# Batch 0's scores and the head of its softmax in two halves of the tokens

## Chip, core and metric

One core of a Trainium2 chip runs the kernel alone. The metric is the device time of one execution in microseconds (us). In the profile of the kernel before, TensorE carries the matrix multiplications and transposes (4265 records), VectorE and ScalarE the work on elements (744 and 415), and SyncE issues the transfers (116). The mean clock that TensorE was granted is its share of full speed, 1.00 being full. Each experiment was timed in rounds beside the kernel before; there were three sets of rounds, on three different chips.

## The reference, cut to what matters

```python
# x: (8, 8, 512, 64), state: (8, 8, 32, 64)
scores = scale * x @ state.T          # softmax over the 32 states
xread  = softmax(scores) @ state
scores2 = scale * state @ x.T         # softmax over the 512 tokens
sread  = softmax(scores2) @ x
# both, concatenated along the tokens -> (4352, 512)
h = y @ w_in                          # 512 -> 2048
out = (h * sigmoid(1.702 * h)) @ w_out
```

## The kernel before

The weights arrive as 8-byte words and are rounded on the chip to fp32 in "pieces". `w_in` has four column blocks of four pieces each. A piece takes a load, a "power" (`L182` on VectorE, then `L187` and `L188` on ScalarE) and four VectorE instructions (`L197` to `L200`). The product of batch 0's state with the first column block, called M, needs pieces 0 to 3. The first useful large matmuls, h, need M and batch 0's softmax.

```python
def att_xT_arriving(b, warm):                # transposes of x, chunk by chunk as it lands
    for c in range(SCH):                     # 4 chunks of 128 tokens
        keep_warm(warm)                      # fillers: matmuls on zeros, results unused
        ps = att_ps([P, NPR, P], ...)
        for j in range(NPR):
            nc.tensor.transpose(ps[:, j], x_heads(b, c, j), ident)
        (nc.scalar.copy if c % 2 else nc.vector.tensor_copy)(A[b]["xT"][...], ps)
...
att_xT_arriving(0, 2)
att_scores(0)
powers_to(2)          # power of piece 1
att_blocks(0)         # L285: 32x32 transposes of the scores
att_x_exp(0)          # L321 maximum, L322 subtraction, L323 exponential
round_to(2, 1)        # power of piece 2, rounding of piece 1
att_x_norm(0)         # L330 sum ... L335
keep_warm(24)
att_state(1)
... transposes of batch 1's x ...
att_scores(1)
keep_warm(24)
powers_to(4)
round_to(NPR, 2)      # pieces 2 and 3
att_M(0, 0)           # M
```

Of the kernel before, what the change touches and what calls it, by code (L numbers as in the profile page):

```python
# [10 lines left out]
FP32 = mybir.dt.float32  # L11
I32 = mybir.dt.int32
U32 = mybir.dt.uint32
AF = mybir.ActivationFunctionType
ALU = mybir.AluOpType
AX = mybir.AxisListType
# [4 lines left out]
def kernel(  # L21
# [30 lines left out]
    nc = tc.nc  # L52

    B, H, S, D = x.shape
    Ns = state.shape[2]
    DM = H * D
    DF = moe_w_in.shape[1]
    P = 128
    NPR = P // Ns
    NG = H // NPR  # L60
# [5 lines left out]
    NB = S // Ns  # L66
    HF, HN = NF // 2, DM // 2
    scale = float(1.0 / np.sqrt(D))
# [10 lines left out]
    apool = ctx.enter_context(tc.tile_pool(name="apool", bufs=1))  # L79
# [4 lines left out]
    psH = ctx.enter_context(tc.tile_pool(name="psH", bufs=2, space=bass.MemoryType.PSUM))  # L84
    psO = ctx.enter_context(tc.tile_pool(name="psO", bufs=4, space=bass.MemoryType.PSUM))
# [3 lines left out]
    def att_ps(shape, name):  # L89
        return psA.tile(shape, FP32, tag="att", name=name)  # L90
# [21 lines left out]
    def keep_warm(n):  # L112
        ps = psH.tile([P, FC], FP32, tag="h", name="warm")
        for _ in range(n):
            nc.tensor.matmul(ps, zeros[:, :P], zeros, start=True, stop=True)
# [17 lines left out]
    def x_heads(b, c, j):  # L133
        return xn[b][:, c, NG * j : NG * (j + 1)].rearrange("q g d -> q (g d)")
# [33 lines left out]
    for i, v in enumerate((8.0 * most, 8.0 * (most - least))):  # L168
        t = konst.tile([P, 1], FP32, name=f"edge_{i}")
# [45 lines left out]
    def powers_to(n):  # L215
        while done["a"] < min(n, len(PIECES)):
            load_weights(done["a"] + 1)
            round_a(done["a"])
            done["a"] += 1

    def round_to(n, ahead=AHEAD):

        while done["b"] < min(n, len(PIECES)):
            powers_to(min(done["b"] + 1 + ahead, max(NFC * NPR, done["b"] + 1)))
            round_b(done["b"])
            done["b"] += 1
            while done["b"] > NPR and done["load"] < len(PIECES) and before(done["load"]) < done["b"]:
                load_weights(done["load"] + 1)
# [12 lines left out]
    A = {b: {} for b in range(B)}  # L241

    def att_state(b):
        ps = att_ps([P, P], f"stT_{b}")
        nc.tensor.transpose(ps, stn[b].rearrange("p g d -> p (g d)"), ident)
        A[b]["stT"] = apool.tile([P, P], FP32, tag="stT", name=f"stT_{b}", bufs=2)
        nc.scalar.copy(A[b]["stT"], ps)
# [9 lines left out]
    def att_xT_arriving(b, warm):  # L257

        A[b]["xT"] = apool.tile([P, NPR, S], FP32, tag="xT", name=f"xT_{b}")
        for c in range(SCH):  # L260
            keep_warm(warm)
            ps = att_ps([P, NPR, P], f"xT_{b}_{c}")
            for j in range(NPR):
                nc.tensor.transpose(ps[:, j], x_heads(b, c, j), ident)
            (nc.scalar.copy if c % 2 else nc.vector.tensor_copy)(A[b]["xT"][:, :, P * c : P * (c + 1)], ps)

    def by_state(b, ps, rhs):

        for j in range(NPR):
            for g in range(NG):  # L270
                rows, st = slice(D * g, D * (g + 1)), slice(Ns * j, Ns * (j + 1))
                nc.tensor.matmul(ps[g][st], A[b]["stT"][rows, st], rhs(rows, j), start=True, stop=True)  # L272

    def att_scores(b):
        a = A[b]
        a["s"] = [psO.tile([P, S], FP32, tag="o", name=f"s_{b}_{g}") for g in range(NG)]
        by_state(b, a["s"], lambda rows, j: a["xT"][rows, j])

    def att_blocks(b):

        a = A[b]
        t = apool.tile([P, NG, NB, Ns], FP32, tag="e1", name=f"e1_{b}")
        a["e1"] = t
        for g in range(NG):
            nc.vector.transpose(t[:, g].rearrange("p i n -> p (i n)"), a["s"][g])  # L285
# [30 lines left out]
    def att_x_exp(b):  # L316

        a = A[b]
        t = a["e1"].rearrange("p g i n -> p (g i) n")
        mx = apool.tile([P, NS1], FP32, tag="mx", name=f"mx_{b}")  # L320
        nc.vector.reduce_max(out=mx, in_=t, axis=AX.X)  # L321
        nc.vector.tensor_tensor(out=t, in0=t, in1=mx.to_broadcast((P, NS1, Ns)), op=ALU.subtract)  # L322
        nc.scalar.activation(out=t, in_=t, func=AF.Exp, scale=scale)  # L323
# [15 lines left out]
    def att_M(b, c, spare=False):  # L339

        m = mpool.tile([P, NG, FC], FP32, tag="M", name=f"M_{b}_{c}")
        A[b]["M", c] = m
        name = f"M_{b}_{c}_"
        ps = [psH.tile([P, FC], FP32, tag="h", name=name + str(g)) if spare else att_ps([P, FC], name + str(g)) for g in range(NG)]
        by_state(b, ps, lambda rows, j: w_in[c][rows, j])
        for g in range(NG):
            nc.scalar.copy(m[:, g], ps[g])  # L347
# [337 lines left out]
    round_to(1, 0)  # L685
    att_state(0)
    att_xT_arriving(0, 2)
    att_scores(0)
    powers_to(2)
    att_blocks(0)  # L690
    att_x_exp(0)
    round_to(2, 1)
    att_x_norm(0)
    keep_warm(24)
# [2 lines left out]
        keep_warm(2)  # L697
        att_xT(1, j)
    att_scores(1)
    keep_warm(24)  # L700
    powers_to(4)
    round_to(NPR, 2)
    att_M(0, 0)
# [130 lines left out]
```

## Time and profile before

| | before |
|---|---|
| time, median of the first 3 runs | 754.42 us (754.26 to 754.55) |
| TensorE, VectorE, ScalarE busy | 738.5, 432.5, 233.1 us of 752.6 |
| mean granted clock, profiled run | 0.999 |
| M starts; h starts | 29.31; 31.15 us |

TensorE is busy 98% of the time, so the end should move with the moment at which its useful work begins. The relevant stretch is the first 43 us; in the timelines, columns are start, duration, engine, line, operation, and in brackets how long the engine was idle before it and what ended that. PE stands for TensorE, DVE for VectorE, ACT for ScalarE. The prediction shows the lines.

### The profile page before, as it was taken

What the parts mean: (1) busy time and instruction counts of PE and PEld (TensorE: products, weight loads), DVE (VectorE), ACT (ScalarE), POOL (GpSimd) and SP (SyncE); (2) the same over time, 40 slices, a digit from 0 to 9 for tenths busy, and PEclk for the clock granted to TensorE, in tenths of its full rate; (3) what the DMA queues carried; (4) which work ended last, traced back from release to release, by engine and by line L of the source; (5) the groups of instructions that cost most, each with busy time, mean ns of one, the idle gap of its engine ahead of it and who ended that gap; (6) DMA issues with size and microseconds to landing.
All of it is one profiled execution on the core that took longest, in us unless ns stands there. A gap on an engine that the chain in (4) does not pass through costs nothing.

```text
span 752.6 us, 10076 instructions
## 1 busy us (share of the span) xinstructions
PE 738.5 (98%) x4265; PEld 564.6 (75%) x4267; DVE 432.5 (57%) x744; ACT 233.1 (31%) x415; POOL 0.8 (0%) x8
## 2 busy tenths in 40 slices
PE   8989999999999999999999999999999999999997
PEld 3433444467888878887788788887888778888996
DVE  5999799642646383645637264638355563762341
ACT  4676511022324241433134232424143313300210
POOL 0000000000000000000000000000000000000000
PEclk9999999999999999999999999999999999999999
DMA  9811245010030000300030003000030000000000
GB/s 234 332 57 56 93 160 144 0 57 1 28 86 4 1 15 31 72 1 15 29 74 0 1 29 84 6 1 15 29 74 1 15 29 15 0 15 29 15 1 28
DMA packets 48764, 35.24 MB, mean 47 GB/s; under 512 B 36432, under 2 KB 44112, under 8 KB 48720
## 3 DMA queue, kind: packets, MB, share of 16 engines
q1 hardware_dynamic: 48720, 34.61, 16.0%
q8 instruction: 33, 0.54, 0.3%
q14 instruction: 11, 0.09, 0.0%
HBM read 25.69 MB, written 8.91 MB: 46 GB/s over the span
## 4 chain that ended last, share of the span: by engine, by line
PE 96%; SPq 2%; ACT 1%; DMA 1%; issue 0%; DVE 0%; ACTq 0%
PE y L483 19%; PE z L483 13%; PE x L483 13%; PE upy L614 8%; PE h L418 8%; PE o L436 7%; PE upz L614 6%; PE upx L614 6%; PE M L272 4%; PE xT L254 2%; PE upy_sr L614 1%; PE y_sr L483 1%; SPq L131 1%; PE sr L367 1%; PE s L272 1%; PE upz_sr L614 1%
## 5 line engine op out<-in xcount | busy, mean ns | idle before, releaser
L483 PE MATMUL x<-w_out,g 128*128 128x256 f32 x448 | 100.2, 379 | 0.0
L483 PEld LDWEIGHTS x<-w_out,g 128*128 128x128 f32 x448 | 84.3, 190 | 11.2 <-ACT osb L443 0.2
L624 DVE TENSOR_TENSOR g<-upy,g 128x512 f32<-128x512 f32 x72 | 48.1, 689 | 68.4 <-PE upy L614 68.4
L621 ACT ACTIVATE g<-g 128x512 f32<-128x512 f32 (+1 forms) x84 | 49.8, 600 | 100.5 <-DVE g L624 100.5
L347 ACT COPY M<-M 128x512 f32<-128x512 f32 x64 | 33.2, 596 | 95.1 <-PE M L272 95.1
L418 PE MATMUL h<-aT,M 128*128 128x512 f32 x128 | 58.2, 600 | 4.4 <-ACT M L347 4.4
L418 PEld LDWEIGHTS h<-aT,M 128*128 128x128 f32 x128 | 23.6, 190 | 36.7 <-issue 24.4
L483 PE MATMUL z<-sums,later 128*128 128x256 f32 x224 | 51.1, 382 | 0.0
L483 PE MATMUL z<-w_out,g 128*128 128x256 f32 x224 | 50.8, 382 | 0.0
L483 PE MATMUL y<-sums,later 128*128 128x256 f32 x224 | 50.5, 379 | 0.0
L483 PE MATMUL y<-sums,g 128*128 128x256 f32 x224 | 50.5, 379 | 0.0
L483 PE MATMUL y<-w_out,g 128*128 128x256 f32 x224 | 50.1, 382 | 0.0
L483 PEld LDWEIGHTS z<-sums,later 128*128 128x128 f32 x224 | 42.1, 190 | 10.4 <-issue 5.0
L483 PEld LDWEIGHTS y<-w_out,g 128*128 128x128 f32 x224 | 42.1, 190 | 10.4 <-issue 5.0
L614 PE MATMUL upx<-aT,M 128*128 128x256 f32 x192 | 49.3, 379 | 0.0
L614 PE MATMUL upy<-ta,M 128*128 128x256 f32 x192 | 49.3, 379 | 0.0
L483 PEld LDWEIGHTS z<-w_out,g 128*128 128x128 f32 x224 | 41.7, 190 | 6.1
L483 PEld LDWEIGHTS y<-sums,g 128*128 128x128 f32 x224 | 41.7, 191 | 5.1
L483 PEld LDWEIGHTS y<-sums,later 128*128 128x128 f32 x224 | 41.7, 191 | 5.1
L500 DVE TENSOR_TENSOR osb<-z,later 128x512 f32<-128x512 f32 x14 | 9.7, 692 | 58.4 <-PE z L483 58.4
L614 PEld LDWEIGHTS upy<-ta,M 128*128 128x128 f32 x192 | 36.5, 190 | 4.9
L614 PEld LDWEIGHTS upx<-aT,M 128*128 128x128 f32 x192 | 36.5, 190 | 4.9
(147 smaller groups left out, 1028.0 us busy)
## 6 DMA issues: line engine op xcount, KB each, us to landing
later<-in_moe_w_out_dram SPq DMA_DIRECT2D x16, 512.0 KB
out_dram<-osb SPq DMA_DIRECT2D x32, 256.0 KB
xn<-in_x_dram SPq DMA_DIRECT2D x28, 256.0 KB
w_out<-in_moe_w_in_dram SPq DMA_DIRECT2D x12, 512.0 KB
later<-in_moe_w_in_dram SPq DMA_DIRECT2D x4, 512.0 KB
sums<-in_x_dram SPq DMA_DIRECT2D x4, 256.0 KB
stn<-in_state_dram SPq DMA_DIRECT2D x16, 32.0 KB
out_dram<-osb_sr SPq DMA_DIRECT2D x4, 128.0 KB
```

The source lines that it names most:

```text
L131: nc.sync.dma_start(xn[b][:, c], x_v[b, c])
L254: nc.tensor.transpose(ps[:, c], x_heads(b, c, j), ident)
L272: nc.tensor.matmul(ps[g][st], A[b]["stT"][rows, st], rhs(rows, j), start=True, stop=True)
L347: nc.scalar.copy(m[:, g], ps[g])
L367: nc.tensor.matmul(ps[st, g], a["eT"][:, g, c, st], xn[b][:, c, NG * j + g], start=(c == 0), stop=(c == SCH - 1),)
L418: nc.tensor.matmul(hps, lhs[i], rhs[i], start=(i == 0), stop=(i == n - 1))
L436: nc.tensor.matmul(ops, G[key, f // 2][:, f % 2, P * r : P * (r + 1)], w_out[:, f], start=(f == 0), stop=(f == NF - 1))
L483: nc.tensor.matmul(ps[:, r], lhs[f][:, P * r : P * (r + 1)], rhs[:, f], start=(first and r == 0 and f == 0), stop=(f == HF - 1), skip_grou ...
L500: nc.vector.tensor_tensor(out=o, in0=ps, in1=with_, op=ALU.add)
L614: nc.tensor.matmul(ps[:, k], lhs[i][:, o : o + P], rhs[i], start=(first and k == 0 and i == 0), stop=(i == n - 1), skip_group_check=True,)
L621: nc.scalar.activation(out=dst, in_=src, func=AF.Gelu_apprx_sigmoid)
L624: nc.vector.tensor_tensor(out=dst, in0=ps, in1=x, op=ALU.add)
```

## The change

While chunks 2 and 3 of batch 0's x are transposed and copied, VectorE was partly idle (0.56 us before 10.15, 1.29 before 12.13, 0.28 before 12.83). The intent is to use that: scores of tokens 0 to 255 and the first part of their softmax right after chunk 1, the rest after chunk 3. VectorE would then be done earlier with batch 0, and with the weight pieces behind it, so ten fillers in front of M are dropped. The fillers in front of chunks 2 and 3 go too, and the copy of chunk 2 moves from VectorE to ScalarE.

```diff
 def att_xT_arriving(b, warm):
     for c in range(SCH):
-        keep_warm(warm)
+        if c < 2:
+            keep_warm(warm)
...
-        (nc.scalar.copy if c % 2 else nc.vector.tensor_copy)(A[b]["xT"][...], ps)
+        (nc.scalar.copy if c else nc.vector.tensor_copy)(A[b]["xT"][...], ps)
+        if c % 2:
+            att_half(b, c // 2)
+
+def att_half(b, i):       # scores, 32x32 transposes, maximum, subtraction of one half
+    ...
 att_xT_arriving(0, 2)
+nc.scalar.activation(out=A[0]["e1"], in_=A[0]["e1"], func=AF.Exp, scale=scale)
 att_scores(0)             # the full scores stay: the other softmax needs them
 powers_to(2)
-att_blocks(0)
-att_x_exp(0)
 round_to(2, 1)
...
 att_scores(1)
-keep_warm(24)
+keep_warm(14)
```

More of the change, by code (lines that the diff above doesn't have):

```diff
@@ L264, in att_xT_arriving @@
                 nc.tensor.transpose(ps[:, j], x_heads(b, c, j), ident)
-            (nc.scalar.copy if c % 2 else nc.vector.tensor_copy)(A[b]["xT"][:, :, P * c : P * (c + 1)], ps)
+            (nc.scalar.copy if c else nc.vector.tensor_copy)(A[b]["xT"][:, :, P * c : P * (c + 1)], ps)
+            if c % 2:
+                att_half(b, c // 2)
     def by_state(b, ps, rhs):
@@ L272, in by_state @@
                 nc.tensor.matmul(ps[g][st], A[b]["stT"][rows, st], rhs(rows, j), start=True, stop=True)
+    def att_half(b, i):
+        a = A[b]
+        if i == 0:
+            a["e1"] = apool.tile([P, NG, NB, Ns], FP32, tag="e1", name=f"e1_{b}")
+            a["mx"] = apool.tile([P, NG, NB], FP32, tag="mx", name=f"mx_{b}")
+        n, w = S // 2, slice(NB // 2 * i, NB // 2 * (i + 1))
+        pool, tag = ((psH, "h"), (psO, "o"))[i]
+        ps = [pool.tile([P, n], FP32, tag=tag, name=f"sh_{b}_{i}_{g}") for g in range(NG)]
+        by_state(b, ps, lambda rows, j: a["xT"][rows, j, n * i : n * (i + 1)])
+        for g in range(NG):
+            nc.vector.transpose(a["e1"][:, g, w].rearrange("p i n -> p (i n)"), ps[g])
+        t, mx = a["e1"][:, :, w], a["mx"][:, :, w]
+        nc.vector.reduce_max(out=mx, in_=t, axis=AX.X)
+        nc.vector.tensor_tensor(out=t, in0=t, in1=mx.to_broadcast((P, NG, NB // 2, Ns)), op=ALU.subtract)
     def att_scores(b):
```

## The prediction

> **What bounds the kernel now.** I read the page first: TensorE is busy 738.5 of 752.6 us, and the chain that ended last is 96% TensorE. So a change at the start pays only by what it moves TensorE's first useful matmuls forward. The change touches nothing after about 31 us; I therefore read the chain of waits, merged and in order of time, from 0 to 70 us:
>
> ```profile
> 15.13 4.25 DMA sums<-in_x_dram
> ...
> 22.36 1.73 PE s L272 x16
> 24.09 0.32 PE warm L115
> ...
> 24.46 4.91 PE warm L115 x22
> 29.38 1.16 PE M L272 x16
> 30.53 0.57 ACT M L347
> ```
>
> The columns are start and duration in us. Batch 1's x lands at about 19.4; its transposes and scores end at 24.09; then 24 filler matmuls run to 29.38, when M of batch 0 starts, the first product on the way to the h matmuls (31.15) and all that follows. Fillers have no input to wait for, so they are on the chain because TensorE has no other work. The question is what M would wait for if they were fewer. M's four row blocks need weight pieces 0 to 3 rounded. The timeline of VectorE says when the last one is ready:
>
> ```profile
> 12.83 1.31 DVE L285 STREAM_TRANSPOSE e<-s 128x512 f32<-128x512 f32 x2 [0.28 <-PE s L272]
> 14.18 1.22 DVE L321 TENSOR_REDUCE mx<-e 128x32 f32<-128x1024 f32 x1
> 15.44 1.23 DVE L322 TENSOR_TENSOR e<-e,mx 128x1024 f32<-128x1024 f32 x1
> 16.58 0.42 DVE L182 TENSOR_SCALAR later<-w_out 128x512 int32<-128x512 int32 x1
> 16.91 0.42 DVE L197 TENSOR_SCALAR w_in<-w_out 128x512 int32<-128x512 int32 x1
> 17.25 0.69 DVE L198 SCALAR_TENSOR_TENSOR later<-w_out,later 128x512 int32<-128x512 int32 x1
> ...
> 19.18 1.21 DVE L330 TENSOR_REDUCE sm<-e 128x32 f32<-128x1024 f32 x1
> ...
> 28.36 0.69 DVE L200 SCALAR_TENSOR_TENSOR w_in<-w_in,later 128x512 f32<-128x512 f32 x1
> ```
>
> No bracket with idle time follows the first of these: VectorE works without a gap from 12.83 on. Piece 3 is done at 28.36 + 0.69 + 0.04 (the handover that the chain shows as "issue") = 29.09, only 0.22 us before M's first matmul (29.31 in the timeline). So two things bind M almost together: fillers and VectorE. Removing fillers is worth what VectorE's chain shortens, and 0.22 us at most if it does not. ScalarE's timeline of the same stretch:
>
> ```profile
> 8.82 0.58 ACT L265 COPY xT<-xT 128x512 f32<-128x512 f32 x1 [1.73 <-PE xT L264]
> 11.02 0.58 ACT L265 COPY xT<-xT 128x512 f32<-128x512 f32 x1 [1.61 <-PE xT L264]
> 12.59 0.72 ACT L187 ACTIVATE later<-later,edge 128x512 f32<-128x512 int32 x1 [0.99 <-DVE later L182]
> 13.35 0.72 ACT L188 ACTIVATE later<-later,edge 128x512 int32<-128x512 f32 x1
> 16.70 1.06 ACT L323 ACTIVATE e<-e 128x1024 f32<-128x1024 f32 x1 [2.63 <-DVE e L322]
> 17.66 0.71 ACT L187 ACTIVATE later<-later,edge 128x512 f32<-128x512 int32 x1
> ```
>
> The reader is to see that L187 and L188 at 12.59 to 14.07 compute piece 1's power beside VectorE's softmax, so that L198 at 17.25 finds it ready, without a wait.
>
> [...]ScalarE sat idle 2.63 us before the exponential with later work behind it.[...] the trace has 0.69 (L200) and 1.23 (L322), so half a softmax step costs 0.53 us less, not half.[...] The trace has 2.12 us of idle TensorE before the h matmuls at 42.17, and its granted clock stays 1.00 there and after.
>
> **The change, part by part.**
>
> First half. Chunk 1's transposes end as before; VectorE's copy of chunk 0 still waits for piece 0's rounding and runs at 8.90, 0.69 long. So the half's scores start at 8.90 + 0.69 + 0.05 = 9.64. A full score step occupies TensorE 1.02 us and its reader starts 1.18 after its start (11.65 to 12.83). Half the columns save half of the 0.85 us of streaming (two passes of 0.427 us, read off the h matmuls: 16 records in 7.13 us, so 0.446 each, less a little), about 0.43. Occupied: 0.60; to the reader: 0.76. VectorE starts at 10.40; two transposes, a maximum, a subtraction: 0.81 + 0.73 + 0.73 = 2.27 to the next engine (from the intervals 1.35, 1.26, 1.26 of the full size, less 0.53 each). It ends near 12.6, in time that was mostly idle before. This is the intended gain.
>
> Second half. Chunk 2's transposes now stand behind the first half's scores: 9.64 + 0.60 = 10.24, not 9.46; chunk 3's follow at 10.68, without fillers between. Both copies are now ScalarE's: 10.90 and 11.39 (back to back 0.49, as the M copies). Scores of the half at 11.39 + 0.58 + 0.05 = 12.02, to VectorE at 12.02 + 0.76 = 12.78, against 12.83 before. Its softmax head takes 2.27 to ScalarE instead of 3.87: the exponential starts at 15.05 instead of 16.70, 1.65 us earlier.
>
> What takes it back. The order of instructions shows that ScalarE's queue changed as well: the exponential now stands ahead of piece 1's L187 and L188, which were in front of it. VectorE's L182 for piece 1 has also moved behind the second half's subtraction. So L187 waits for the exponential: 15.05 + 0.96 = 16.01 (the interval 16.70 to 17.66), L188 + 0.75 = 16.76, and L198 + 0.75 (6.21 to 6.96 for piece 0) = 17.51. VectorE is through with two L182 and one L197 at 12.78 + 2.17 + 3 x 0.34 = 15.97, so it stalls 1.5 us in front of L198. L198 started at 17.25 before: it is 0.26 us LATER. From there VectorE's list is the same as before up to piece 3, with no wait by the trace: ready at 29.09 + 0.26 = 29.35.
>
> TensorE. The full scores of batch 0 remain (they serve the other softmax), so the two halves add 1.2 us of matmuls; with 24 fillers it reaches batch 1's work at about 18.75 + its state's transpose, still before x of batch 1 at 19.4. Scores of batch 1 end near 24.15, fillers 14 x 0.216 = 3.0 us later at 27.2. Three of M's row blocks go at once (piece 2 is done at 26.7); the fourth waits for 29.35. It then takes as long as all eight matmuls: in batch 1's scores the last pair began after its copy at 23.04 and the next work on TensorE at 24.09, 1.05 us, against 1.02 for eight together.[...] So M ends at about 29.35 + 1.05 = 30.40, as before (29.38 + 1.02 = 30.40). The 2.1 us of fillers removed become a wait for VectorE. ScalarE copies M, h starts at 31.15, and everything behind follows unchanged: batch 1's softmax is 0.26 us later, done at 40.3, needed at 42.17; M of the next column block needs piece 7, done at 48.0, at 49.2.
>
> Sum: 0.0 us, give or take 0.3.
>
> **Rivals.**
> First, VectorE does not stall, and its 1.6 us of saved time reach M: then M would start when the fillers end, 27.2 to 27.5, and the time be 752.4 to 752.9. For it: the idle time before 12.83 is really used. Against: the position of the exponential in ScalarE's queue. It needs piece 1's power ready by 15.97, which the queue cannot give.
> Second, the second half comes later than I have it, because chunk 2's transposes wait for the first half's scores and two copies queue on one engine. Each tenth there is a tenth on L198 and on M: with 0.4 us more, 754.8.
> Third, fewer fillers let the clock drop. TensorE is nearly idle from 8.6 to 12.0 and from 28.2 to 29.35, then 0.75 more before h.[...] The 2.12 us idle at full clock speak against it, and M's matmuls lie in between.
>
> **Range and chances.** The median of before is 754.42; I predict 754.4. Below: the second half may be 0.2 us earlier, and the remaining pair of M may be 0.1 quicker than eight, and a part of the stall may not be there: 753.7. Above: 0.3 us of timing, 0.2 of the kernel's own spread, some of the clock: 755.1. Two per cent is 15 us, half of all that happens before 31 us; both sides get 0.01.
>
> **What would show it.** VectorE's timeline: an idle of about 1.5 us before L198 near 17.5, ended by ScalarE's L188, and norm (the second reduction) starting near 19.4, not 17.8. The first half's head between 10.4 and 12.6. The exponential near 15.05. TensorE: idle of about 1 us inside M, ended by VectorE's L200, and h at 31.15 within 0.3. Granted clock 1.00 throughout. The prediction is wrong if L198 starts before 17 (the first rival), or if h moves by more than half a microsecond.

The forecast's sum came to 0.0 us, give or take 0.3: 754.4, within 753.7 to 755.1. What no trace before it showed is cut, at the marks: a rule on the order of instructions, a formula for VectorE's times, a rule on the clock, a reason why M's last pair takes as long as all eight, and, of the third rival, a length of half clock with the 1.7 us (756) that followed from it. No term of the sum goes with them. How the rest stands without them:

- "What takes it back" rests on VectorE and ScalarE keeping their order. That was my assumption.
- The 0.53 us that half a step saves came from the formula. The trace of the kernel before has 1.23 less 0.69, 0.54; the changed kernel's has 0.78 for the pair of transposes, 0.69 and 0.69, against 1.31, 1.22 and 1.23: 0.53, 0.53 and 0.54.
- The 0.427 us is my estimate from the h matmuls of the kernel before: 16 records take 7.13 us and 12 take 5.42, so four more take 1.71, 0.4275 each. The two passes are the two records that the trace lists for each of a step's 8 matmuls. That half the columns save half of it was an estimate too. The changed kernel's half step occupies TensorE for 0.60 us (9.63 to 10.23).
- "Some of the clock" in the upper end, about 0.2 us, is an allowance that no trace gave.

## The result, and the profile after

The changed kernel took 754.84 us in the median of 4 runs (754.01 to 755.68), the kernel before 754.48 in 4 runs of its own (754.26 to 755.70). The ratio is 1.0001, with a 95% interval of 0.9983 to 1.0020: the same. A ratio here is the mean time of one kernel's runs over that of the other's of the same rounds, so it is not quite the ratio of the medians.

VectorE's timeline of the changed kernel, the lines that answer to those of the prediction (line numbers have moved: L285 is L288, L330 is L349):

```profile
10.38 0.78 DVE L288 STREAM_TRANSPOSE e<-sh 128x256 f32<-128x256 f32 x2 [0.89 <-PE sh L275]
...
12.80 0.78 DVE L288 STREAM_TRANSPOSE e<-sh 128x256 f32<-128x256 f32 x2 [0.20 <-PE sh L275]
...
14.34 0.69 DVE L291 TENSOR_TENSOR e<-e,mx 128x512 f32<-128x512 f32 x1
14.95 0.77 DVE L182 TENSOR_SCALAR later<-w_out 128x512 int32<-128x512 int32 x2
15.64 0.42 DVE L197 TENSOR_SCALAR w_in<-w_out 128x512 int32<-128x512 int32 x1
17.52 0.69 DVE L198 SCALAR_TENSOR_TENSOR later<-w_out,later 128x512 int32<-128x512 int32 x1 [1.46 <-ACT later L188]
...
19.46 1.21 DVE L349 TENSOR_REDUCE sm<-e 128x32 f32<-128x1024 f32 x1
...
28.65 0.69 DVE L200 SCALAR_TENSOR_TENSOR w_in<-w_in,later 128x512 f32<-128x512 f32 x1
```

The first half's work stands at 10.38, where VectorE was idle before. The subtractions are finished at 15.03, against 16.67 before. Then comes an idle time of 1.46 us in front of L198, ended by ScalarE's L188. L198 starts at 17.52; before it was 17.25. ScalarE's timeline shows why:

```profile
10.92 1.07 ACT L266 COPY xT<-xT 128x512 f32<-128x512 f32 x2 [1.62 <-PE xT L265]
15.06 1.07 ACT L707 ACTIVATE e<-e 128x1024 f32<-128x1024 f32 x1 [3.07 <-DVE e L291]
16.04 0.70 ACT L187 ACTIVATE later<-later,edge 128x512 f32<-128x512 int32 x1
16.77 0.72 ACT L188 ACTIVATE later<-later,edge 128x512 int32<-128x512 f32 x1
```

ScalarE is idle for 3.07 us, then runs the exponential, and only then piece 1's power, which VectorE is waiting for. In those 3.07 us the power could not have run, though, because its first instruction, L182, ran on VectorE only at 14.95, behind the second half's subtraction; in the kernel before it ran at 12.13. TensorE's timeline, first one line of the kernel before, then the changed kernel from M on:

```profile
42.17 7.13 PE L418 MATMUL h<-aT,M 128*128 128x512 f32 x16 [2.12 <-ACT M L347]
```

```profile
24.32 3.19 PE L115 MATMUL warm<-sums 128*128 128x512 bf16 x14
27.45 1.07 PE L275 MATMUL M<-w_in,stT 64*32 64x512 f32 x12
29.39 1.05 PE L275 MATMUL M<-w_in,stT 64*32 64x512 f32 x4 [0.87 <-DVE w_in L200]
31.11 7.13 PE L437 MATMUL h<-aT,M 128*128 128x512 f32 x16 [0.67 <-ACT M L366]
42.14 8.83 PE L437 MATMUL h<-aT,M 128*128 128x512 f32 x16 [2.12 <-DVE w_in L199]
```

The fillers end 1.9 us earlier (27.51 against 29.37), and the last row block of M waits for VectorE's piece 3. h starts at 31.11 against 31.15. So far the change is worth nothing. The last line is a surprise. The second group of h matmuls takes 8.83 us; its neighbour of the same 16 matmuls takes 7.13, and so does the same group in the kernel before. The table of stretches has the granted clock in the third column from the end, the value after the counts of POOL; first the kernel before, then the changed kernel:

```profile
43.00:44.00 1.00, 1.00 (x4) 0.39 (x3) 1.00 (x4) 0.00 (x0) 0.00 (x0) 1.00 0.03 8
```

```profile
43.00:44.00 1.00, 1.00 (x3) 0.39 (x2) 1.00 (x3) 0.00 (x0) 0.00 (x0) 0.60 0.10 25
44.00:45.00 1.00, 1.00 (x3) 0.48 (x2) 0.96 (x3) 0.05 (x1) 0.00 (x0) 0.50 0.00 0
45.00:46.00 1.00, 1.00 (x2) 0.38 (x2) 0.97 (x3) 1.00 (x2) 0.00 (x0) 0.50 0.00 0
46.00:47.00 1.00, 1.00 (x3) 0.35 (x2) 1.00 (x4) 0.88 (x2) 0.00 (x0) 0.70 0.00 0
```

(The row ends with clock, share of the DMA engines, and GB/s.) Asked for by itself, the stretch from 43.20 to 46.60 has a clock of 0.50, the 1.06 us in front of it 1.00 and the 0.40 us behind it 0.99. The lost clock adds up to 0.40 + 0.50 + 0.50 + 0.30 = 1.70 us, which is what the group is longer by. The profiled execution of the changed kernel was one of its two runs near 755.6 at a mean clock of 0.996 or 0.997; the other two took 754.07 and 754.01 at 0.999. So there are two kinds of runs, told apart by the mean clock that TensorE was granted. The kernel before has both kinds too: 755.7 was one of its first four (in later rounds such times stand at 0.996 or 0.997). Kernels must therefore be compared within one kind, by the mean clock of each run: 0.998 to 1.000 in the one kind, 0.994 to 0.997 in the other.

### The profile page after: what moved, and what is told of

Its sections match the earlier page's. It is cut to its first block, busy times and chain, and to the rows that moved or that the text cites. A ratio compares the mean times of both kernels' runs of the same rounds, so it can differ in the third digit from the quotient of the medians. Undisturbed runs are those within 1.5% of the kernel's fastest.

```text
span 753.9 us, 10117 instructions
## 1 busy us (share of the span) xinstructions
PE 740.0 (98%) x4285; PEld 563.8 (75%) x4285; DVE 432.6 (57%) x747; ACT 233.7 (31%) x416; POOL 0.8 (0%) x8
## 4 chain that ended last, share of the span: by engine, by line
PE 94%; DVE 4%; ACT 1%; DMA 1%; issue 0%; ACTq 0%
PE y L502 19%; PE z L502 13%; PE x L502 13%; PE upy L633 8%; PE o L455 7%; PE h L437 7%; PE upx L633 5%; PE upz L633 5%; PE M L275 4%; PE upy_sr L633 1%; PE xT L254 1%; PE y_sr L502 1%; PE sr L386 1%; PE upz_sr L633 1%; PE upx_sr L633 1%; PE z_sr L502 1%
## 5 line engine op out<-in xcount | busy, mean ns | idle before, releaser
L437 PE MATMUL h<-aT,M 128*128 128x512 f32 x128 | 59.9, 614 | 4.3 <-ACT M L366 2.2
```

Source lines behind the costliest of these rows:

```text
L437: nc.tensor.matmul(hps, lhs[i], rhs[i], start=(i == 0), stop=(i == n - 1))
```

## The experiments

Ten runs. Two questions: was VectorE's gain taken back by the new order of piece 1's power and the exponential, and what halves the clock?

### Piece 1's power in front of the exponential

```diff
             (nc.scalar.copy if c else nc.vector.tensor_copy)(A[b]["xT"][...], ps)
+            if c == SCH - 1:
+                powers_to(2)
             if c % 2:
                 att_half(b, c // 2)
```

> Piece 1's power (L182 on VectorE, then L187 and L188 on ScalarE) put between the two halves, so that it stands in front of the exponential on ScalarE. Theory (the gain was taken back by ScalarE's queue): no stall before piece 1's L198, which starts near 15.8 instead of 17.5; the second reduction near 17.7 instead of 19.46; M's last pair near 27.6 instead of 29.39, h near 29.35 instead of 31.11; quickest runs 1.75 us below the changed kernel's 754.05, so 752.3. Rival (something other than the power is what VectorE waits for, or M is bound by x of batch 1): no change, 754.0.

Measured: 752.46 us in the median of 5 (752.21 to 753.76), ratio 0.9965 (0.9952 to 0.9978) to the kernel before. Four runs at a clock of 0.999 took 752.21 to 752.74, the fifth 753.76 at 0.997; the five runs of the kernel before at 0.999 in the same rounds took 754.07 to 754.38. Its timelines of ScalarE, VectorE and TensorE:

```profile
13.67 0.72 ACT L188 ACTIVATE later<-later,edge 128x512 int32<-128x512 f32 x1
15.05 1.06 ACT L709 ACTIVATE e<-e 128x1024 f32<-128x1024 f32 x1 [0.66 <-DVE e L293]
```

```profile
12.46 0.42 DVE L182 TENSOR_SCALAR later<-w_out 128x512 int32<-128x512 int32 x1
...
15.61 0.69 DVE L198 SCALAR_TENSOR_TENSOR later<-w_out,later 128x512 int32<-128x512 int32 x1
```

```profile
27.47 1.09 PE L277 MATMUL M<-w_in,stT 64*32 64x512 f32 x16
29.32 7.13 PE L439 MATMUL h<-aT,M 128*128 128x512 f32 x16 [0.75 <-ACT M L368]
```

L198 no longer waits and starts 1.9 us earlier; h starts 1.79 us earlier; the quickest run is 1.8 us below the changed kernel's quickest. The exponential itself is not later than in the changed kernel (15.05 against 15.06), because it waits for VectorE's subtraction anyway (0.66 us here, 3.07 there). L182 now runs at 12.46, between the halves, and L187 and L188 fit into ScalarE's idle time. The place of three instructions, one on VectorE and two on ScalarE, was what took the gain back.

### Only the exponential moved behind the power

```diff
-nc.scalar.activation(out=A[0]["e1"], ..., func=AF.Exp, scale=scale)
 att_scores(0)
 powers_to(2)
+nc.scalar.activation(out=A[0]["e1"], ..., func=AF.Exp, scale=scale)
```

> Only the exponential moves behind piece 1's L187 and L188 on ScalarE; VectorE's list is that of the changed kernel. Theory: L187 starts when VectorE's L182 is done, 15.38, L198 near 16.87 instead of 17.52, so 0.65 us of the 1.7 come back: quickest runs near 753.4. Rival (the place of the exponential alone was the cause): L198 near 15.9 and the whole 1.6 us, 752.4. Second rival (the second reduction must wait for the later exponential, which then takes the place of the stall): no gain.

Measured: 755.06 us in the median of 5, ratio 0.9993; four of the five runs were of the kind with the lower mean clock (755.03 to 755.23 at 0.997), the one at 0.999 took 753.51. VectorE's line in its profile:

```profile
16.85 0.69 DVE L198 SCALAR_TENSOR_TENSOR later<-w_out,later 128x512 int32<-128x512 int32 x1 [0.87 <-ACT later L188]
```

L198 came to 16.85 (expected 16.87), and M's last row block to 28.70. Here a wait of 0.87 us remains, because L182 for piece 1 still stands behind the second half on VectorE. So the exponential's place alone gives back 0.67 us of L198's delay (17.52 less 16.85); the other 1.2 us came back only with L182 moved as well. L182 moved alone was not run; with the exponential still ahead, L187 would by ScalarE's order start no earlier than the 16.04 of the changed kernel, so my estimate is no gain from it. The two moves belong together. In the median this run looks like a failure; only the clock beside each time shows that it is not.

### The fillers in front of M

The changed kernel with `keep_warm(24)` again, and the kernel before with `keep_warm(14)`:

> The changed kernel with 24 fillers again in front of M. Theory: M waits for VectorE's piece 3 (29.36), the fillers would now end at 24.35 + 24 x 0.216 = 29.53, so M is at most 0.2 us later and all eight of its matmuls run after it: quickest runs 754.1 to 754.3. Rival (the fewer fillers are what keeps the change from losing): 2 us slower, 756.

Measured: 754.55 us in the median of 6; the four at 0.999 took 754.25 to 754.57, two at 0.997 took 755.76 and 756.21. M starts at 29.34 in its profile, when the fillers end and piece 3 is ready (28.60 + 0.69 + 0.04 = 29.33). By the times the ten fillers cost 0.2 to 0.6 us in the changed kernel (against 754.01 and 754.07, from other rounds), slightly more than expected, and not 2. The traces show only 0.07 us of that (h at 31.18 against 31.11); the rest is open.

> The kernel before with 14 instead of 24 fillers in front of M, and nothing else. Theory: VectorE has piece 3 ready at 29.09, so M's last pair starts there instead of 29.31 with a pair as long as all eight: at most 0.2 us quicker, full-clock runs 754.1 to 754.4. Rival (the fillers alone were the bound, and removing them is the part of the change that should have gained): 752.3. Second rival (the fillers keep the clock up): more runs at the lower mean clock of 0.997, near 755.9, than the kernel before in the same rounds.

Measured: 755.36 us in the median of 5; two at 0.999 took 753.94, three at 0.996 took 755.36 to 755.75. TensorE's timeline of this kernel:

```profile
26.95 1.07 PE L272 MATMUL M<-w_in,stT 64*32 64x512 f32 x12
29.05 1.05 PE L272 MATMUL M<-w_in,stT 64*32 64x512 f32 x4 [1.03 <-DVE w_in L200]
```

The kernel before, too, waits for VectorE when its fillers are fewer. Going from 24 to 14 alone is worth about 0.4 us (753.94 against 754.31 to 754.43 at full clock in the same rounds), slightly more than the 0.2 that I expected. Part of the difference is that h follows the start of the last 4 records of M by 1.72 us (29.05 to 30.77), but the start of all 16 by 1.84 (29.31 to 31.15 in the kernel before). Three of five runs at the lower clock against six of nine of the kernel before in the same rounds says nothing against the 14.

### The gap in front of the second group of h

```diff
     att_x_norm(1)
     att_M(1, 0)
+    keep_warm(8)
```

in the changed kernel:

> The changed kernel with 8 more fillers behind M of batch 1's first column block, in the gap of 2.12 us before the h matmuls at 42.14. Theory (the half clock from 43.2 to 46.6 in the profiled run of 755.68 comes from the gap[...]): all runs near 754.0, none near 755.6, clock 1.00 from 43 to 47. Rival (the clock falls for another reason, or earlier, from the fewer fillers): two kinds of runs as before, 754.0 and 755.6.

in the kernel before:

> The kernel before with the 8 fillers in the same gap. Theory (the gap is what costs 1.6 us in about half of its executions): full-clock runs 754.2 as before, at most one in five near 755.9. Rival (the place[...] is by chance whatever the gap): about half near 755.9.

What is cut out of the two is a mechanism of the clock that no trace shows.

Measured: the changed kernel 754.00 us in the median of 6, five between 753.92 and 754.07, one at 755.59 (0.996). The kernel before 754.31 in the median of 5 (754.00 to 754.82), all at 0.999 or 1.000. TensorE's timeline of the changed kernel with the gap filled:

```profile
40.13 1.67 PE L115 MATMUL warm<-sums 128*128 128x512 bf16 x7 [0.16 <-issue]
42.09 7.13 PE L437 MATMUL h<-aT,M 128*128 128x512 f32 x16 [0.28 <-ACT M L366]
```

The h matmuls start where they did and take 7.13 us; the idle time before them is 0.28 instead of 2.12 us. In the three sets of rounds the kernel before lost its clock in 16 of 29 runs (6 of 11, 6 of 9 and 4 of 9, all at 0.996 or 0.997; one more, 755.41 at 0.998, is not counted). That this gap is the main place is shown in two ways. In five kernels with it filled (these two and three below), 1 of 26 runs in the same rounds stood at 0.997 or less; the pair that differs in the fillers alone is the kernel before, 0 of 5 with them and 6 of 9 without. And the three profiled runs at 0.997 with the gap open (the changed kernel, the exponential alone moved, the 24 fillers) all have a clock of 0.50 in the group behind the gap; by their tables of stretches it cost 1.70, 1.71 and 1.71 us there. Why the one of the 26 lost its clock is open; it was not profiled. The sixth kernel with the gap filled, the one without fillers below, is left out of this count, because it loses its clock earlier.

### Both, and a second gap

Piece 1's power first together with the filled gap; then also `keep_warm(6)` behind `att_M(0, 1)`:

> Piece 1's power first (the quickest so far, 752.2) together with 8 fillers in the gap behind M of batch 1. Theory: the two do not touch one another; 752.1 to 752.3 in nearly all runs, none or one at a mean clock of 0.997 and 753.8. Rival (the fillers delay the h matmuls or the mode of the clock has nothing to do with this gap): 752.3 and 753.8 in the same shares as the kernel before has its two kinds.

> As the run with both, and 6 more fillers in the next gap (1.5 us behind M of batch 0's second column block). Theory (the one run in six that still lost its clock lost it in this second gap): all runs within 752.0 to 752.4 at a clock of 0.999. Rival (it is lost elsewhere, for instance where TensorE transposes chunks of x before 12 us): about one in six still 1.6 us longer.

Measured: 752.47 us (752.13 to 753.11), ratio 0.9963, and 752.51 (752.30 to 753.27), ratio 0.9964, five runs each. No run lost its clock (0.998 to 1.000), but neither kept within the 0.2 to 0.4 us that I had named, and the second gap added nothing. The profiled run with both was the slow one, 753.11 at a clock of 1.00. TensorE's and VectorE's lines of it say what it waited for:

```profile
20.65 0.33 PE L254 MATMUL xT<-ident,sums 128*128 128x128 f32 x1 [0.47 <-DMA sums<-in_x_dram]
```

```profile
22.77 0.43 DVE L182 TENSOR_SCALAR later<-w_out 128x512 int32<-128x512 int32 x1 [0.53 <-DMA w_out<-in_moe_w_in_dram]
```

Once the stall is gone, the landings of batch 1's x and of weight piece 4 reach the path (waits of 0.47 and 0.53 us above), and they vary: the profiled run with 6 fillers, below, lists neither wait. Here M started at 28.37 instead of 27.47, behind the fillers that followed the late x; piece 3 was ready shortly before, at 27.38 + 0.69 + 0.04 = 28.11. The delay is 0.9 us, and 753.11 less 752.21 is the same.

### Fewer fillers, and none

The kernel with both, with 6 and with 0 instead of 14 fillers in front of M:

> As the run with both (power first, gap filled), with 6 instead of 14 fillers in front of M. In the profiled run of that kernel VectorE waited 0.53 us for weight piece 4 to land and TensorE 0.72 us for x of batch 1. Theory (landings are now the bound beside VectorE's list): the quickest runs stay at 752.1, since piece 3 is ready at 27.4 there and 14 fillers end at 27.5; late ones gain at most 0.3 us, so runs between 752.0 and 752.9. Rival (the fillers still bound it): all runs 1.7 us less, 750.5. Second rival (the fillers hold the clock up): runs near 753.8 at 0.997.

> The same without any filler in front of M. Theory: as with 6, 752.0 to 752.9, since TensorE only waits longer for VectorE. Rival (an idle stretch[...] on TensorE halves the clock behind it, as the gap behind M of batch 1 did): about half of the runs near 753.8 at 0.997.

A length in the rival, from which on an idle stretch would halve the clock, is cut: no trace shows one.

Measured with 6: 752.28 us (752.13 to 752.70), ratio 0.9961 (0.9947 to 0.9974). With none: 753.86 (753.75 to 755.09), ratio 0.9986; every run at a clock of 0.994 or 0.996. TensorE's timeline without fillers, then the stretch from its table:

```profile
27.58 1.05 PE L277 MATMUL M<-w_in,stT 64*32 64x512 f32 x4 [1.55 <-DVE w_in L200]
29.30 8.83 PE L439 MATMUL h<-aT,M 128*128 128x512 f32 x16 [0.67 <-ACT M L368]
```

```profile
30.00:32.00 2.00, 2.00 (x4) 0.88 (x3) 1.97 (x5) 0.71 (x1) 0.00 (x0) 0.50 1.02 418
```

M's last row block and h start within 0.1 us of where they do with 6 fillers (27.68 and 29.40), but the first group of h takes 8.83 us. My expectation fell, and the rival that I had named was right, in all five runs and not in half of them: the fillers do not set when M's last row block starts, but without any the clock behind it fell (0.50 in the stretch above). With six it stayed at 1.00 in the profiled run, from 28 to 44 us, and the mean was 0.998 to 1.000 in all five runs. Two of the five runs without fillers stood at 0.994 and were another 1.2 to 1.3 us longer (755.07 and 755.09); where they lost that is open. The version with 6 has the lowest median of all kernels here, but only by 0.2 us, less than the spread of its runs; that it is quicker than the version with 14 is not shown. Against the kernel before it gains 0.4% over both kinds of runs, part of which is the clock; against that kernel's full-clock runs of the same rounds (754.30 to 754.44, and one of 754.93) it is about 2 us, 0.3%.

## Why the prediction was right, and where it was not

**The time.** I predicted 754.4 and 753.7 to 755.1; the median was 754.84. The full-clock runs, 754.01 and 754.07, are within the range; the two near 755.6 are above it. The range held the median of a mixture of two kinds that I did not know of. That was partly luck: with one more run of the slow kind among the four, the median would have been near 755.6.

**VectorE's gain and its loss.** The times were right step by step. The exponential was expected at 15.05 and started at 15.06; L198 at 17.51, measured 17.52; the stall 1.5, measured 1.46; h at 31.15, measured 31.11. A small error hides in it: the first half's scores came 0.15 us behind the copy, not 0.05, while the whole trace was 0.1 us earlier. The experiments show the cause: putting the power first gives the 1.8 us back, and moving the exponential alone gives 0.67 us. The prediction names both moves, the exponential ahead of L187 and L182 behind the subtraction, but argues against its first rival with the place of the exponential alone. By the runs that was not the whole cause: with the exponential out of the way, only 0.67 of the 1.9 us at L198 came back, because L182 still stood late on VectorE.

One reading was weaker than I took it for. ScalarE's 2.63 us of idle time in the kernel before, which I quoted for ScalarE's order, does not show that later work waits in order, because that work was not ready: its L182 ran on VectorE only at 16.58. The run with the exponential alone moved does show it. There the subtraction was done at 14.97 (14.28 + 0.69), yet ScalarE stayed idle until L187 at 15.34 and ran the exponential at 16.73, behind L187 and L188.

**M's last pair.** I expected that four records take as long as sixteen. The trace has 1.05 us for 4 and 1.09 us for 16; why is not shown. From their start to h it is 1.72 us for 4 (29.39 to 31.11) and 1.84 for 16 (29.31 to 31.15). This 0.12 us, which the range had allowed for, is why h came 0.04 us earlier although M's last row block started 0.08 later.

**The first rival** (the saved time reaches M) was rightly refused for the change as written, and is what the first experiment made true.

**The third rival, the clock.** Here a step failed. I argued that "The 2.12 us idle at full clock speak against it", from one execution of the kernel before. In 16 of 29 later runs of that kernel the clock was lower, and filling that very gap all but cured it (1 of 26). The size that I had named was met by the profile: 1.70 us for 3.4 us at 0.50. The chance was wrong, because one profile cannot show what half of the executions do. The place that I feared, 31 us, kept its clock in the profiled runs with 24, 14 and 6 fillers (7.13 us for the group) and lost it in the one with none (8.83 us, 0.50); all five runs with none had a lower mean clock. The stretch from 8.6 to 12.0, called nearly idle, was idle for 0.95 + 0.73 us only and kept its clock (1.00 from 8 to 12 us). "Granted clock 1.00 throughout" was thereby wrong for the profiled run. That the change altered the chance is not shown: 2 of 4 after against 1 of 4 before is too few.

## What to carry to other kernels

When work is moved ahead on one engine, read the new order on that engine and on every one that answers it. Here a short instruction that another engine needed (L182) had slipped behind the moved work, and a long one that waits (the exponential) stood in front of what followed; together they gave the whole gain away without any engine being busier. Before a few tenths of a per cent are read as a gain or a loss, sort the runs by their clock, since one gap of 2.12 us before a dense group cost 1.7 us here in the runs that lost their clock, as much as the change had to give. Fillers can be free where another engine is awaited and still not removable: here 14 and 6 took the same time within the spread (medians 752.47 and 752.28), and none took 1.6 us more than 6 (753.86). Try several numbers, zero too.

## What these runs show of the clock

- The clock fell to 0.50 behind an idle gap of 2.11 or 2.12 us in three profiled runs (mean clock 0.997). It stayed at 1.00 behind a gap of 2.12 us in two others, the kernel before and the one with the power first (mean clock 0.999); the kernel before had a lower mean clock in 16 of 29 runs. Without fillers it fell after idle stretches of 0.45, 1.55 and 0.67 us amid small matmuls in the profiled run, and all five runs had a lower mean clock. In the changed kernel's profile the half clock lasted 3.4 us (43.20 to 46.60). What decides whether it falls is not shown.
- How many fillers suffice was found by trying. In front of the first h group 6 did and 0 did not; behind M of batch 1, with 8 the lower clock came in 1 of 26 runs of five kernels, against 16 of 29 of the kernel before.
